# A linear-attention and squared-ReLU kernel: batch 0's attention in halves of the heads, batch 1's turns moved from TensorE to DMA, and one of batch 2's loads made to wait

## The chip, the cores and the metric

The kernel runs on one core of a Trainium2 chip. The metric is the device time of one execution in microseconds, the median of several runs. TensorE is called PE, VectorE DVE, ScalarE ACT, GpSimd POOL, and SyncE (which here only issues DMAs) SP.

## The reference

The inputs are q, k and v of 8 batches, 8 heads, 576 positions and 64 channels, and two weights, w1 (512 x 2048) and w2 (2048 x 512), all in float32. Position s has the angle pi/2 * s/576.

```python
def phi(x, c, s):                       # c, s: cosine and sine of the position
    r = np.maximum(x, 0.0)
    return np.concatenate([r * c, r * s], axis=-1)          # 128 features a head
q_p, k_p = phi(q, cos_w, sin_w), phi(k, cos_w, sin_w)
kv  = np.einsum('bhsf,bhsd->bhfd', k_p, v)
z   = np.sum(k_p, axis=2)
num = np.einsum('bhsf,bhfd->bhsd', q_p, kv)
den = np.einsum('bhsf,bhf->bhs', q_p, z)[..., None] + 1e-06
x   = (num / den)                        # heads side by side: 4608 rows of 512
h   = x @ w_in
r   = np.maximum(h, 0.0)
out = (r * r) @ w_out
```

## The kernel before

Work goes by batches. A batch has 576 positions: four tiles of 128 (j = 0 to 3) and a tail of 64 (j = J = 4). Its attention is made of these steps, each a declared operation:

- loads: `k`, `v`, `q` of the batch, 1 MB each, and their tails `kt`, `vt`, `qt`, two transfers of 64 KB each. There is one buffer for each name, so a batch's load waits until the batch before has read it.
- features: for every j the cosine half and the sine half of k and of q (`relu_scale`, L407 on DVE, L405 on ACT), and a cast of v to bfloat16 beside a column of ones (`vx`, L412).
- the product of k's features and v with its ones, `kz`, summed over j, and a copy of it, `kvz`.
- the turn of q's features, so that the feature lies on the partitions: for batches 2 to 7 by DMA transposes on SP (`declare_qT`, L567), for batch 1 and batch 0 by PE against an identity with a copy out of PSUM (`declare_qT_pe`, L580; in the prologue L1107).
- numerator and denominator in one product, `num`, and the division on DVE (`div`, L626 to L628).
- the turn of the result x to `xT`: for batches 2 to 7 by DMA transposes (`declare_xT`, L656), for batch 1 and 0 by PE (`declare_xT_pe`, L668; prologue L1135).

After it come the first product of the two-layer part, `x @ w1`, its ReLU on ACT and square on DVE, and the second product with w2. Batches 0 to 2 do the first product plainly (`declare_plain`); batch 0 does the second one by rows (`declare_rows`, 64 matmuls of 512 columns, which use w2 quarter by quarter); later ones use a scheme with seven block products in place of eight. Almost all matmuls are recorded at L429, the helper `mm`.

The order on the engines is not written by hand, except for the prologue. Every operation is declared with the engines that may do it, its duration, what it reads and writes, and for PE a place in time (`pos`). A planner then walks through time: it picks on each engine what can start first, and among equals what is due first, gives out the buffers, and so makes a fixed instruction order for each engine. `SHIFTS`, a string of "operation number : shift", moves the due times of single operations, and sometimes fixes an engine. On the chip every engine works through its list in order and waits where it must. Operations called `given` tell the planner when something that it does not place itself will be ready.

Before the planner's part stands `prologue` (L1057), written out by hand: it issues batch 0's loads (k on SP, the others on POOL's queue), the constants, the four loads of w1 (L372, `load_w1`), and does the attention of batch 0's first two tiles for all heads at once. While PE has nothing to do, it is kept busy by matmuls on zeros (L1069, L1101, L1132), whose results nobody reads. Tiles 2, 3 and the tail of batch 0 are declared for the planner. POOL's queue then loads w2 in quarters (L379) and batch 1:

```python
    declare_load(1, "q", "POOL", 17.0)
    declare_w2_load(0, 19.0, 10.0)
    declare_load(1, "k", "POOL", 20.0)
    declare_w2_load(1, 22.0, 11.0)
    declare_load(1, "v", "POOL", 23.0)
    declare_w2_load(2, 25.0, 12.0)
    declare_w2_load(3, 26.0, 13.0)
```

and after batch 1's attention, in the declared order, batch 2's q, k and v, also on POOL. w1 and w2 are converted to bfloat16 by the transfer. Batches 3 to 7 are loaded from SP.

Of the kernel before, what the change touches and what calls it, by code (L numbers as in the profile page):

```python
# [21 lines left out]
21:4.5 31:1.0 44:-3.0 53:1.5 60:1.0 74:3.0 80:2.0 93:-7.5 105:-0.5 132:-2.5 134:2.0 146:-7.0  # L22
149:-8.5 153:-6.5:ACT 178:4.0 181:-2.5 192:32.0 198:-6.0 206:3.0 215:-1.5 236:3.0 252:18.5
255:10.5 257:20.5 260:-2.5 261:18.5 263:3.0 264:-1.0 296:-16.5 300:-26.0 313:4.0 315:-1.5
335:-1.5 339:-6.0 350:-3.5 390:5.0 392:4.0 411:3.5 440:66.0 446:-7.5 467:6.5:DVE 470:13.5:DVE
486:-2.5 500:3.0 527:4.0 559:1.5 566:1.0 569:1.0 571:0.5 575:3.5 578:-2.0 581:-2.0 583:1.0
587:3.0 608:-3.5 609:1.0 619:-1.5 620:8.5 625:4.5 628:9.0 632:-49.0 644:-1.0 646:1.5:ACT 653:1.0
670:8.5 675:9.0 683:5.5 700:2.5 725:-4.0 727:-4.5 729:2.5 731:6.0 755:-4.5 759:-2.5 761:-1.5
762:-2.0 777:6.0 783:1.0 789:-1.0 799:-3.0 804:3.0 806:-5.0 807:-5.0:ACT 810:-5.5:ACT 814:33.5
818:-5.5 827:8.0 828:-29.5 833:5.5 835:-9.5 848:-7.0 854:12.5 873:0.5 913:-2.0 915:1.5 927:3.5  # L30
928:13.5 947:1.5 955:-15.0 964:-3.0 973:4.0 1003:-25.5 1005:4.0 1010:4.0 1012:4.5 1015:2.0
1036:5.0 1072:11.5 1151:7.0 1156:9.0 1169:-3.5 1218:2.5 1278:-1.5 1330:-1.0 1335:3.0
# [18 lines left out]
class Planner:  # L51
# [23 lines left out]
    def add(self, engs, fn, r=(), w=(), pos=None, lat=None, size=None, after=(), land=2.2, held=None):  # L75
# [5 lines left out]
        op.land, op.held = land, held  # L81
# [45 lines left out]
    def plan(self, t0):  # L127
# [7 lines left out]
        for o in pe:  # L135
            o.late = o.slot = t
            t += o.engs["PE"]
# [37 lines left out]
        while left:  # L175
# [32 lines left out]
            if o.size:  # L208
                pipe = max(o.end + o.land, pipe) + o.size
                o.done = pipe + self.margin  # L210
                if o.held is not None:
                    o.end = max(o.end, pipe - o.held)
# [19 lines left out]
def kernel(  # L232
# [120 lines left out]
    def load_main(src, nm, i, b, eng, parts=1):  # L353
        main = mem[nm][:, i]
        for n in range(parts):
            js = slice(n * J // parts, (n + 1) * J // parts)
            eng.dma_start(
                out=main[:, :, js, :],
                in_=src[b, :, 0:MAIN, :].rearrange("h (p j) d -> p h j d", j=J)[:, :, js, :],
            )  # L360
# [74 lines left out]
    LOAD = 3.4  # L435
# [10 lines left out]
    T1, T2, t = {}, {}, 16.8  # L446
# [11 lines left out]
    def declare_load(b, nm, eng, pos=None, after=()):  # L458
        src = {"k": k, "v": v, "q": q}[nm]
        queue = nc.sync if eng == "SP" else nc.gpsimd  # L460
        for part, fn, cost, size in ((nm, load_main, 0.7, LOAD), (nm + "t", load_tail, 1.4, 0.4)):
            buf = loaded[part, b] = plan.buf(part)

            def load(_, fn=fn, buf=buf):
                fn(src, nm, buf.i, b, queue)

            add((eng, cost), load, w=[buf], pos=pos, size=size, after=after)

    def source(nm, b, j):
        return loaded[nm if j < J else nm + "t", b]  # L470

# [27 lines left out]
    def declare_feature(nm, b, j, part, engs):  # L499
# [4 lines left out]
        cost = {"ACT": 0.63 * n, "DVE": 0.40 * n}  # L504
# [5 lines left out]
        add({e: cost[e] for e in engs}, feature, r=[source(nm, b, j)], w=[(buf, j % 2, part)])  # L510
# [11 lines left out]
    def declare_kz(b, pos, engs=("ACT",)):  # L522
        ba, bb = plan.buf("F"), plan.buf("F")
        kvz = kvzb[b] = plan.buf("kvz")
        for j in range(NS):

            def kz(_, j=j):
# [18 lines left out]
                ("PE", T_MM65 * (2 * HH)),  # L546
# [47 lines left out]
    def declare_num(b, j, pos):  # L594
# [22 lines left out]
        add(("PE", T_MM65 * 2 * HH), num, r=[qT, kvzb[b]], w=bks, pos=pos)  # L617
# [75 lines left out]

    def declare_plain(b, hb, half, pos, split=False):
# [3 lines left out]
        for c in range(2) if split else (None,):  # L698

            def plain(_, c=c):  # L700
# [13 lines left out]
                r=[(xT, i) for i in ((0, 1) if c is None else (c,))] + [("w1", hb // 4)],  # L714
# [77 lines left out]
    def declare_seven1(b, r, t):  # L792
# [12 lines left out]
        def product(name, off, acc, w, x, first, reads):  # L805
# [27 lines left out]
            ("DVE", 0.6), lambda _: add_relu(block(1, 1), halves(bank(E)), halves(at(u3))),  # L833
# [4 lines left out]
            ("DVE", 0.6), lambda _: add_relu(block(0, 1), halves(bank(E)), halves(at(u2))),  # L838
# [65 lines left out]
    def declare_pair(b, pair, t):  # L904
# [7 lines left out]
        for n, ops, op, reads in (  # L912
# [5 lines left out]
            add(("DVE", 0.6), lambda _, n=n, ops=ops, op=op: sub(at(gs[n]), *ops(), op), r=reads, w=[gs[n]])  # L918
# [92 lines left out]
    def declare_att(b, kpos, npos, cos_k="B", cos_q="D", cast="A"):  # L1011
        EN = {"B": BOTH, "A": ACT1, "D": DVE1}
        cos_k, cos_q, cast = (EN.get(x, x) for x in (cos_k, cos_q, cast))
# [5 lines left out]
        for j in range(NS):  # L1019
            declare_feature("q", b, j, "c", cos_q)  # L1020
            declare_feature("q", b, j, "s", ACT1)
            if b > 1 and (j == J or j % 2):
                declare_qT(b, j // 2)
            elif b == 1:
                declare_qT_pe(b, j, npos[j] - 3.5, DVE1)
        for j in range(NS):
            declare_num(b, j, npos[j])
            if b > 1 and (j == J or j % 2):
                declare_xT(b, j // 2)
            elif b == 1:  # L1030
                declare_xT_pe(b, j, npos[j] + 2.0, BOTH)
# [10 lines left out]
    loaded["k", 0] = bind(plan.buf("k"), 0, 9.5)  # L1042
    loaded["v", 0] = bind(plan.buf("v"), 0, 12.0)
    loaded["q", 0] = bind(plan.buf("q"), 0)
    loaded["kt", 0] = bind(plan.buf("kt"), 0, 9.5)
    loaded["vt", 0] = bind(plan.buf("vt"), 0, 12.0)
    loaded["qt", 0] = bind(plan.buf("qt"), 0)
    for j in range(NS):
        bind(kp_of(0, j), j if j < J else 0, 12.5)
        bind(cached(vxb, (0, j), "vx" if j < J else "vxt"), j if j < J else 0, 12.5)  # L1050
    kvzb[0] = bind(plan.buf("kvz"), 0)
    bind(qp_of(0, 0), 0, 13.6)
    bind(x_of(0, 0), 0, 16.8)
    bind(xT_of(0, 0), 0)
    qTp0 = [bind(plan.buf("qpTp"), j, 14.6) for j in range(2)]

    def prologue():  # L1057
        nc.vector.memset(zeros, 0.0)
        for t, n in (("vx", D), ("vxt", D)):
            m = mem[t]  # L1060
            nc.vector.memset(m[:, :, :, D:E1], 1.0)
        load_main(k, "k", 0, 0, nc.sync)
        load_tail(k, "k", 0, 0, nc.gpsimd)
        load_main(v, "v", 0, 0, nc.gpsimd)
        load_tail(v, "v", 0, 0, nc.gpsimd)
        constants()
        load_main(q, "q", 0, 0, nc.gpsimd, 2)
        for i in range(31):
            nc.tensor.matmul(out=banks[:, i % 2, :], lhsT=zeros[:, 0:P], rhs=zeros, start=True, stop=True)  # L1069
        for j in range(NS):  # L1070
            kp = at(kp_of(0, j))
            relu_scale("DVE", kp[:, :, 0:D], piece("k", 0, j), cos_col[:, j : j + 1])
            relu_scale("ACT", kp[:, :, D:F], piece("k", 0, j), sin_col[:, j : j + 1])
        for j in range(NS):
            copy("ACT" if j == 1 else "DVE", at(vxb[0, j])[:, :, 0:D], piece("v", 0, j))
        for i in range(4):
            load_w1(i, 4)
        load_tail(q, "q", 0, 0, nc.gpsimd)
        kz = banks[:, 6:8, :]
        for j in range(NS):  # L1080
            for hh in range(HH):
                for half in range(2):
                    h = half * HH + hh
                    kp, vx = at(kp_of(0, j)), at(vxb[0, j])
                    if j < J:
                        lhsT, rhs = kp[:, h, :], vx[:, h, :]
                    else:
                        p0, p1 = half * TAIL, (half + 1) * TAIL
                        lhsT, rhs = kp[p0:p1, hh, :], vx[p0:p1, hh, :]
# [163 lines left out]
```

## Time and profile before

| | us |
|---|---|
| runs | 279.13, 279.6, 278.8; median 279.13 |
| the profiled execution's own time | 278.33 |
| its span, first to last instruction | 276.6 |
| PE / DVE / ACT / POOL busy | 269.0 / 219.1 / 192.6 / 28.4 |
| granted clock of PE | 1.00 |
| first matmul with w1 starts | 18.49 |
| last matmul ends | 272.6 |

Busy times are sums of recorded instructions; matmuls overlap in the pipeline, so their spacing, as the chain of waits gives it, says more than their recorded durations of some 0.2 to 0.3 us. In the chain a matmul of 128 columns takes 0.056 us, and eight of 256 columns take 0.87 us. The DMA's "busy share" can exceed 1 in a window, since more than one packet of an engine can be under way.

In the first 18 us the engines work on batch 0's attention, and the loads landed as follows (time of issue and time to landing by the trace): k 6.25, v 9.8, q's two halves 11.46 and 12.98, the quarters of w1 at 16.1, 18.0, 20.5 and 23.1. Then on the same queue: the first w2 quarter at 26.8, batch 1's q at 29.4, its k at 32.0, the second w2 quarter at 34.4, batch 1's v at 37.6, the third and fourth w2 quarter at 40.7 and 43.3, batch 2's q, k and v at 46.2, 49.2 and 52.6.

### The profile page before, as it was taken

The numbers are of one execution on the slowest core, as the hardware profiler recorded it, in microseconds if no ns is written. First come the engines' busy times: TensorE is split into PE (matmuls) and PEld (weight loads), VectorE is DVE, ScalarE is ACT, GpSimd is POOL, SyncE is SP. The second block draws the span as 40 slices with busy tenths as digits, with TensorE's granted clock in tenths as the row PEclk, the third lists the DMA queues.
The fourth block names the chain that finished last, engine by engine and source line by source line (L and its number), as shares of the span: only waits on it lengthen the run. The fifth ranks groups of instructions, "written<-read, shape, count | busy, mean of one in ns | idle before, by whom it ended". The sixth has DMA issues, their size and how long they took to land.

```text
span 276.6 us, 7125 instructions
## 1 busy us (share of the span) xinstructions
PE 269.0 (97%) x2846; PEld 227.8 (82%) x2851; DVE 219.1 (79%) x515; ACT 192.6 (70%) x385; POOL 28.4 (10%) x46
## 2 busy tenths in 40 slices
PE   8979999999999999999999999999999999999994
PEld 3658856789888988888888888988988888888883
DVE  1849996998795896799977999799946997279741
ACT  3767862798798796499848995699738643685421
POOL 8925244100000000000000000000000000000000
PEclk9999999999999999999999999999999999999999
DMA  7999999776999999899899428997583301200024
GB/s 228 311 206 287 330 256 374 220 174 148 368 191 257 281 248 238 220 331 160 237 266 377 114 40 167 330 219 210 57 233 77 94 32 42 112 1 2 8 88 134
DMA packets 77824, 53.01 MB, mean 192 GB/s; under 512 B 52032, under 2 KB 73024, under 8 KB 77792
## 3 DMA queue, kind: packets, MB, share of 16 engines
q1 hardware_dynamic: 70368, 37.63, 54.7%
q0 software_dynamic: 7280, 14.81, 19.8%
q8 instruction: 22, 0.36, 0.5%
q10 hardware_dynamic: 144, 0.13, 0.1%
q14 instruction: 10, 0.08, 0.1%
HBM read 36.70 MB, written 9.44 MB: 167 GB/s over the span
## 4 chain that ended last, share of the span: by engine, by line
PE 81%; DVE 11%; DMA 2%; issue 2%; POOL 2%; ACT 1%; POOLq 0%; DVEq 0%
PE banks L429 78%; DVE gT L418 3%; DVE rs L421 3%; DVE gs L426 3%; DMA q<-in_q_dram 2%; PE banks L580 1%; DVE gTt L418 1%; PE banks L668 1%; PE banks L1132 1%; ACT qp L405 1%; POOL kt L365 1%; DVE x L628 1%; POOL vt L365 0%; ACT sums L412 0%; DVE kp L407 0%
## 5 line engine op out<-in xcount | busy, mean ns | idle before, releaser
L429 PEld LDWEIGHTS <-w1sb 128*128 128x128 bf16 x784 | 72.7, 98 | 8.7
L429 PE MATMUL banks<-xT,w1sb 128*128 128x256 bf16 (+1 forms) x576 | 68.3, 267 | 0.1
L429 PEld LDWEIGHTS <-gs 128*128 128x128 bf16 x512 | 49.5, 98 | 7.0 <-DVE gs L426 0.7
L429 PE MATMUL banks<-w2sb,gT 128*128 128x256 bf16 (+1 forms) x284 | 44.8, 295 | 0.2 <-issue 0.2
L429 PEld LDWEIGHTS <-gT 128*128 128x128 bf16 x400 | 37.4, 98 | 7.5
L415 ACT ACTIVATE rt<-banks 128x512 bf16<-128x512 f32 x64 | 37.2, 602 | 9.2 <-PE banks L429 4.5
L429 PEld LDWEIGHTS <-w1s 128*128 128x128 bf16 x320 | 30.6, 98 | 3.9 <-issue 0.2
L429 PE MATMUL banks<-w2sb,gs 128*128 128x256 bf16 x256 | 32.7, 273 | 0.1
L429 PE MATMUL banks<-w2s,gs 128*128 128x256 bf16 x256 | 32.1, 273 | 0.1
L421 DVE CUSTOM_DVE_ANT_0 rs<-banks,sums 128x512 bf16<-128x512 f32 x40 | 27.0, 684 | 3.8 <-ACT sums L829 3.1
L418 DVE TENSOR_TENSOR gT<-rs 128x1024 bf16<-128x1024 bf16 (+1 forms) x50 | 28.0, 580 | 1.2 <-ACT rs L415 0.6
L426 DVE TENSOR_TENSOR ysb<-banks,sums 128x256 f32<-128x256 f32 x32 | 13.5, 422 | 17.6 <-PE banks L429 9.4
L418 DVE TENSOR_TENSOR gT<-rt 128x512 bf16<-128x512 bf16 x48 | 19.4, 420 | 7.1 <-ACT rt L415 7.0
L415 ACT ACTIVATE rs<-banks 128x512 bf16<-128x512 f32 x40 | 23.5, 606 | 2.0 <-PE banks L429 1.8
L405 ACT ACTIVATE kp<-k,sin_col 128x512 bf16<-128x512 f32 x32 | 22.4, 725 | 0.5 <-DMA k<-in_k_dram 0.5
L429 PE MATMUL banks<-xT,w1s 128*128 128x256 bf16 x160 | 22.7, 273 | 0.0
L429 PE MATMUL banks<-xs,w1s 128*128 128x256 bf16 x160 | 22.7, 273 | 0.0
L405 ACT ACTIVATE qp<-q,sin_col 128x512 bf16<-128x512 f32 x32 | 22.0, 720 | 1.0 <-DMA q<-in_q_dram 1.0
L426 DVE TENSOR_TENSOR gs<-gT 128x1024 bf16<-128x1024 bf16 x28 | 19.2, 689 | 3.1 <-PE banks L429 2.7
L628 DVE TENSOR_TENSOR x<-banks,den 128x512 bf16<-128x512 f32 x30 | 20.7, 691 | 1.0
L429 PE MATMUL banks<-xTt,w1sb 128*128 128x256 bf16 x128 | 16.1, 273 | 0.0
L407 DVE TENSOR_SCALAR kp<-k,cos_col 128x512 bf16<-128x512 f32 x26 | 12.0, 501 | 5.0 <-DMA k<-in_k_dram 5.0
(105 smaller groups left out, 362.8 us busy)
## 6 DMA issues: line engine op xcount, KB each, us to landing
out_dram<-ysb SPq DMA_DIRECT2D x13, 512.0 KB, 3.6
k<-in_k_dram SPq DMA_DIRECT2D x6, 1024.0 KB, 6.4
v<-in_v_dram SPq DMA_DIRECT2D x5, 1024.0 KB, 7.5
q<-in_q_dram SPq DMA_DIRECT2D x5, 1024.0 KB, 9.3
v<-in_v_dram POOLq DMA_DIRECT2D x3, 1024.0 KB, 8.2
w1sb<-in_moe_w_in_dram POOLq DMA_DIRECT2D x4, 512.0 KB, 10.9
w2sb<-in_moe_w_out_dram POOLq DMA_DIRECT2D x4, 512.0 KB, 12.4
q<-in_q_dram POOLq DMA_DIRECT2D x2, 1024.0 KB, 9.1
```

Source lines behind the costliest of these rows:

```text
L365: eng.dma_start(out=tail[g * TAIL : (g + 1) * TAIL, :, :], in_=src[b, g * HH : (g + 1) * HH, MAIN:S, :].rearrange("h p d -> p h d"),)
L405: nc.scalar.activation(out=dst, in_=src, func=ACTF.Relu, scale=col)
L407: nc.vector.tensor_scalar(out=dst, in0=src, scalar1=0.0, scalar2=col, op0=ALU.max, op1=ALU.mult)
L415: nc.scalar.activation(out=out, in_=in_, func=ACTF.Relu)
L418: nc.vector.tensor_tensor(out=out, in0=in_, in1=in_, op=ALU.mult)
L421: nc.vector._custom_dve(TENSOR_ADD_SAT, out=out, in0=in0, in1=in1, s0=float("inf"), s1=0.0)
L426: nc.vector.tensor_tensor(out=out, in0=in0, in1=in1, op=op)
L429: nc.tensor.matmul(out=out, lhsT=lhsT, rhs=rhs, start=start, stop=stop, skip_group_check=True)
L580: nc.tensor.transpose(t[:, h, :], qp_at(b, j)[:, h, :], ident[:, :])
L628: nc.vector.tensor_tensor(out=x_at(b, j).rearrange("p (b k) (l d) -> p b k l d", b=n, l=2), in0=n4[:, :, :, 0:D].rearrange("p b (k l) d -> ...
L668: nc.tensor.transpose(t[:, kb, :], x_at(b, j)[:, kb, :], ident[:, :])
L1132: nc.tensor.matmul(out=banks[:, 6 + i % 2, :], lhsT=ident[:, :], rhs=zeros, start=True, stop=True)
```

## The change

1. *Batch 0's loads* are all issued from SP's queue in one order: k, k's tail, the first half of q (tiles 0 and 1), v's tail, v's heads 0 to 3, v's heads 4 to 7, the second half of q, q's tail. POOL makes both feature halves of k's tile 3. A one-element copy on POOL, from v's first half into w1's buffer, stands ahead of the four w1 loads, so these, and all behind them on POOL, are issued when that half of v has landed.
2. *Batch 0's first two tiles* are declared for the planner (`declare_first`) rather than written out, and in two halves g of the heads: casts of v, products `kz` (the tail first), the copy `kvz`, numerators, divisions and the turns of x are each made for heads 0 to 3 and heads 4 to 7 apart. The planner starts at 8.0 on PE in place of 16.8. Fill matmuls on zeros: 28 ahead and 7 between.
3. *Batch 1* is turned like the later batches, by DMA transposes on SP: two of q's main tiles and one of the tail, the same for x. Its 36 q transposes and 18 x transposes on PE go, with their copies.
4. *POOL's loads* are in another order: w2 quarter 0, batch 1's q, w2 quarter 1, batch 1's k and v, w2 quarters 2 and 3, then batch 2. In the instruction order as built batch 2 follows as k's tail, q, q's tail, v, v's tail, and k's main load last; ahead of that one stands a one-element copy on POOL that reads batch 1's x, tiles 2 and 3, so it is issued after batch 1's last main division.
5. Several planner durations and all of `SHIFTS` are new, so the order of later stages changes on every engine too.

```diff
 SHIFTS = """
-21:4.5 31:1.0 44:-3.0 53:1.5 60:1.0 74:3.0 80:2.0 93:-7.5 105:-0.5 132:-2.5 134:2.0 146:-7.0
...
+7:-0.5 22:3.0:ACT 31:1.5 59:5.0 65:-1.0 68:6.0 71:-3.0 80:0.5 85:-2.0 130:14.5 135:1.0 143:2.5
...
-        for part, fn, cost, size in ((nm, load_main, 0.7, LOAD), (nm + "t", load_tail, 1.4, 0.4)):
+        for part, fn, cost, size in ((nm, load_main, 0.7, size), (nm + "t", load_tail, 1.4, 0.4)):
             buf = loaded[part, b] = plan.buf(part)
 
             def load(_, fn=fn, buf=buf):
+                if gate and fn is load_main:
+                    nc.gpsimd.tensor_copy(out=at(buf)[0:1, 0, 0, 0:1], in_=x_at(*gate)[0:1, 0, 0:1])
                 fn(src, nm, buf.i, b, queue)
...
-            if b > 1 and (j == J or j % 2):
+            if j == J or j % 2:
                 declare_qT(b, j // 2)
-            elif b == 1:
-                declare_qT_pe(b, j, npos[j] - 3.5, DVE1)
         for j in range(NS):
             declare_num(b, j, npos[j])
-            if b > 1 and (j == J or j % 2):
+            if j == J or j % 2:
                 declare_xT(b, j // 2)
-            elif b == 1:
-                declare_xT_pe(b, j, npos[j] + 2.0, BOTH)
...
     def prologue():
+        for src, nm, part in (
+            (k, "k", 0), (k, "kt", 0), (q, "q", 0), (v, "vt", 0), (v, "v", 0), (v, "v", 1), (q, "q", 1), (q, "qt", 0)
+        ):
+            if nm[1:]:
+                load_tail(src, nm[0], 0, 0, nc.sync)
+            elif nm == "k":
+                load_main(src, nm, 0, 0, nc.sync)
+            elif nm == "q":
+                load_main(src, nm, 0, 0, nc.sync, [slice(part * J // 2, (part + 1) * J // 2)])
+            else:
+                h = slice(part * HH, (part + 1) * HH)
+                nc.sync.dma_start(
+                    out=mem["v"][:, 0, h],
+                    in_=v[0, h, 0:MAIN, :].rearrange("h (p j) d -> p h j d", j=J),
+                )
...
-        load_main(k, "k", 0, 0, nc.sync)
-        load_tail(k, "k", 0, 0, nc.gpsimd)
-        load_main(v, "v", 0, 0, nc.gpsimd)
-        load_tail(v, "v", 0, 0, nc.gpsimd)
         constants()
-        load_main(q, "q", 0, 0, nc.gpsimd, 2)
-        for i in range(31):
-            nc.tensor.matmul(out=banks[:, i % 2, :], lhsT=zeros[:, 0:P], rhs=zeros, start=True, stop=True)
...
+        fill(28)
+        for c, col in ((0, cos_col), (D, sin_col)):
+            nc.gpsimd.tensor_scalar(
+                out=at(kp_of(0, J - 1))[:, :, c : c + D], in0=piece("k", 0, J - 1),
+                scalar1=0.0, scalar2=col[:, J - 1 : J], op0=ALU.max, op1=ALU.mult,
+            )
+        nc.gpsimd.tensor_copy(out=w1sb[0:1, 0, 0:1], in_=mem["v"][0:1, 0, 0, 0, 0:1])
         for i in range(4):
             load_w1(i, 4)
-        load_tail(q, "q", 0, 0, nc.gpsimd)
...
+    ORDER1 = []
+    pos = 21.0
+    for nm in "0q1kv23KQV":
+        if nm != "-":
+            ORDER1.append((pos, nm))
+        pos += 1.0 if nm == "-" else 2.65 if nm in "0123" else 3.1
...
+    def declare_transfers(order):
+        for pos, nm in order:
+            if nm in "kvqKVQ":
+                b = 2 - nm.islower()
+                declare_load(b, nm.lower(), "POOL", pos, size=2.7, gate=(1, 3) if nm == "K" else None)
+            else:
+                declare_w2_load(int(nm), pos, 10.0)
...
-    t0 = {"PE": 16.8, "ACT": 17.3, "DVE": 17.1, "SP": 10.0, "POOL": 20.0, "GIVEN": 0.0}
+    t0 = {"PE": 8.0, "ACT": 6.3, "DVE": 6.3, "SP": 10.0, "POOL": 14.2, "GIVEN": 0.0}
```

The core of `declare_first`, for one half g of the heads (casts, product, copy; numerators, divisions and turns of x follow in the same manner):

```python
        for g in range(2):
            hs = slice(g * HH, (g + 1) * HH)
            for i in range(2):                      # cast(): v's heads hs, tiles 2i and 2i + 1
                add({"ACT": 0.6, "DVE": 0.55}, cast, r=[(L("v"), g)],
                    w=[(vxb[0, j], g) for j in (2 * i, 2 * i + 1)])
            for j in (J, *range(J)):                # kz(): four products, one a head
                add(("PE", T_MM65 * HH + 0.02), kz,
                    r=[(kp_of(0, j), j % 2, c) for c in "cs"] + [(vxb[0, j], g) if j < J else vxb[0, j]],
                    w=[ks[g]], pos=12.0 + g + 0.01 * ((j + 1) % NS))
            add({"ACT": 0.35, "DVE": 0.4}, kvz_copy, r=[ks[g]], w=[(kvzb[0], g)])
```

## The prediction

> **What bounds the kernel now.** I read the page's first two parts, then PE's waits and the chain, then the DMA windows, because the change moves work from PE to the DMA queues.
>
> ```profile
> PE 269.0 (97%) x2846; PEld 227.8 (82%) x2851; DVE 219.1 (79%) x515; ACT 192.6 (70%) x385; POOL 28.4 (10%) x46
> PE   8979999999999999999999999999999999999994
> DMA  7999999776999999899899428997583301200024
> ```
>
> PE is busy in every slice after the first few, and the DMA engines are full at the same time for the first 50 us. The stretch from PE's first batch product work to its last matmul:
>
> ```profile
> 18.03:272.65 254.62, 253.93 (x2728) 220.18 (x2732) 209.23 (x489) 182.72 (x368) 16.36 (x23) 1.00 0.74 189
> ```
>
> The first two numbers are the stretch and PE's busy time: 0.7 us of idleness in 254.6. So from 18.03 on only fewer PE instructions can save time; ahead of it an earlier start can. The chain there, and PE's one real wait:
>
> ```profile
> 17.25 0.73 ACT qp L405
> 17.99 0.05 issue
> 18.03 0.62 PE banks L580 x8
> 18.65 1.34 PE banks L429 x24
> 19.99 0.45 PE banks L580 x8
> ...
> PE banks L580 <- ACT qp L405: 1.3, 1, 1.3
> ```
>
> PE stands still for 1.3 us because a q transpose is queued ahead of the first w1 product and its sine half is late on ACT. Eight transposes take 0.45 us in the chain, so 0.056 us each.
>
> The DMA side, 14 to 38 us, then a single large transfer transpose alone on the ring (53.4 to 56.0) and a pair in sequence (88 to 90):
>
> ```profile
> DMA  9999999999999999999999999999999999999999
> DMA packets 4121, 6.67 MB, mean 278 GB/s; under 512 B 240, under 2 KB 3254, under 8 KB 4118
> ...
> DMA packets 2070, 0.52 MB, mean 201 GB/s; under 512 B 2070, under 2 KB 2070, under 8 KB 2070
> ...
> DMA packets 1974, 0.50 MB, mean 249 GB/s; under 512 B 1974, under 2 KB 1974, under 8 KB 1974
> ```
>
> No slice is free between 14 and 38 us. A q transpose (0.52 MB in 256 B packets) fills all engines for 2.0 (88 to 90) to 2.6 us (53.4 to 56). And the load that matters later:
>
> ```profile
> 29.65 0.76 POOL L379 DMA_DIRECT2D w2sb<-in_moe_w_out_dram  x1 [1.97 <-DMA q<-in_q_dram]
> w2sb<-in_moe_w_out_dram POOLq DMA_DIRECT2D x1, 512.0 KB, 11.0
> ...
> 44.32 1.46 PE L429 MATMUL banks<-w2sb,gT 128*128 128x512 bf16 x6
> ```
>
> The third quarter of w2 is issued at 29.65 and lands 11.0 later, at 40.7; PE first uses it in the group at 44.3. So 3.6 us of slack.
>
> **What the Trainium skill says.** "DMA: Bandwidth & Descriptors", section "Queues, rings and completion order": an engine alternates between queues packet by packet, draining a packet of several descriptors before it switches. No window of this trace has a transpose and a POOL load both backed up, so the share each gets is unknown here. Its "Rules for kernel authors" says that issuing from several engines adds no bandwidth, since all share the same 16; the full windows agree. "TensorE: Matmul & The Clock Gate", "Part 1: The HAM clock gate": PE falls to half clock after about 3.4 us of idleness; the trace shows a clock of 1.00 throughout, with no such gap to test it. "Part 4: PE-mode transpose": its output lies in PSUM and needs a copy; the trace shows them (0.69 us on DVE for eight heads).
>
> **The change part by part.**
>
> *Batch 1's transposes.* PE loses 32 + 4 q transposes and 16 + 2 x transposes: 54 x 0.056 = 3.0 us, all of it on the path (PE idles 0.7 in 254.6). Their copies go too (DVE about four of 0.69 and some of 0.41, ACT two or three of 0.58); hidden under PE, worth nothing by themselves.
>
> *Head.* Batch 0's loads all go to SP's queue, in order of need, v in two halves of heads. My chain: k lands at 6.25 as before. Half a megabyte takes 1.5 us (q's two halves landed at 11.46 and 12.98), a tail pair some 0.5. So with k's tail, half of q and v's tail ahead, the halves of v land at 6.25 + 0.5 + 1.5 + 0.5 + 1.5 = 10.3 and at 11.8 (before v landed whole at 9.8), the rest of q at 13.3, its tail at 13.8. The first half is cast by 11.1, multiplied and copied by 12.4; the second is cast by 12.9, its product done by 13.5. Then ACT's queue decides: kv copy 0.4, two q sines 1.33, x copy 0.3, tail sine 0.5, the 8-head copy 1.0, x copy 0.3 = 17.3, so the first w1 product starts at about 17.4, against 18.03 for PE's queue head before. By then PE has also done 16 transposes and 8 numerator products that before came after 18.03: 0.90 + 0.24 = 1.14. Gain 0.6 + 1.14 = 1.7. Bounds: 2.7 (if the 8-head copy's 1.0 is off the path) and 0.7 (if as much is added). The two k features on POOL (by the skill's "GPSIMD Engine Reference", section 3.1, POOL takes 1.96 times as long as DVE; with DVE's 0.57 an estimate of 1.1 us each) end by about 9, two us before use: nothing. SP issues its twelve transfers in 0.46 (main) and 0.6 to 0.7 us (tail) each, by about 8.3 and each before its turn on the engines. The fill matmuls wait for nothing and hold no one up.
>
> *Gate on w1.* POOL's tiny copy waits for v's first half, and the four w1 loads, w2 and batch 1's loads are queued behind it on POOL: issue moves from 7.96 to about 10.4. The queue is fed again about when batch 0's loads end, so what counts is the end of batch 0: the last piece of q landed at 12.98, and now the q tail is ahead of w1 too, at 13.8. All of w1, w2 and batch 1 come 0.8 later, 1.0 with some slip at the change of queue. The last w1 quarter, landed at 23.1, then comes at 24.1 where PE would want it at 17.4 + 6.2 = 23.6: 0.5 lost, but absorbed by the next wait.
>
> *Transfers for batch 1.* Added on SP: two q transposes (2.0 to 2.6 us of all engines each), a small one (0.5), and for x half of that. They start when batch 1's q (29.4 before, about 30.5 now) has its features, about 32 to 34, in the middle of the full stretch, and ahead of them POOL still has k, v and half of w2 to bring. The three q transposes cost 4.5 to 5.7 if nothing overlaps. The third w2 quarter lands at 40.7 + 1.0 + (0 to 5.7) = 41.7 to 47.4. I take 3.5 of it, 45.2: the last transpose partly falls behind that quarter, and POOL's cast loads leave a little room. PE wants that quarter earlier than before: 44.3 - 1.7 (head) - 1.34 (24 q transposes gone) + 0.48 (two numerators now ahead) = 41.8. It waits 45.2 - 41.8 = 3.4. Batch 1's v is on the same queue just ahead and gates PE's kv product likewise; its wait lies inside this one. Behind the waiting PE stand the rows, the numerators, batch 1's divisions, and its x transposes.
>
> *Hold on batch 2.* Only k's main load waits for the division; q and v are ahead of it in POOL's queue, and behind it only two stores. With the last w2 quarter at about 48, three loads at 2.6 each (the distance of such landings before: q 29.4, k 32.0), and x's transposes of about 2.2, k lands near 58; PE's first product with it was at 68.3, now 67. Nothing. ACT has a batch 2 q sine queued ahead of the last row copy, so a late q would block it: 0 to 1.6, taken as 0.
>
> *The new shifts* reorder every later stage. PE's idleness there is already tiny, so at best 0.3, at worst 1.5; taken as 0.
>
> **Sum:** -3.0 - 1.7 + 3.4 = **-1.3 us** on the profiled execution: 278.33 becomes 277.0 (span 276.6 to 275.3). The median of the runs is 279.13, 0.8 above that execution, so 277.8.
>
> **Rivals.** (1) *The transfers ride free*: loads and transposes overlap, the quarter lands at 42, and 0.3 of waiting is left. Gain 4.7 - 0.3 = 4.4, 274.7. For: the engines move 278 GB/s at full busy, and up to 400 in other windows. Against: busy is full either way. (2) *Strictly additive*: the quarter lands between 46.5 and 47.4, the wait is 4.7 to 5.6, and the gain is eaten: 0 to +0.9, 279.5. (3) *Starved transposes, slower*: if a ring with large packets keeps the engines, the w2 quarter comes early, at about 43 (wait 1.3), and q's second transpose, wanted 1.3 later, at 44.4, stays behind v, the rest of w2 and batch 2's q. It decides from a landing at about 47.8, where both waits together reach the 4.7 gained; at 50 they are 1.3 + 5.6 = 6.9, net +2.2, and half clock after such a gap some 0.8 more: +3.0, 282.1. For: queues full; q and v of batch 2 are not held. Against: many small tail loads on POOL's queue give turns to SP's. (4) *The hold does nothing*: k would have come last anyway; 0 either way, inside the above.
>
> **How the numbers follow.** Case 1 has 0.20; my case 0.33 (of it 0.05 within the bound); additive 0.12, of it 0.10 within; starved or a later stage upset 0.35. A measurement of this kernel can tell about 0.3% (0.8 us) from no change. Faster 0.20 + 0.28 = 0.48, same 0.15, slower 0.35 + 0.02 = 0.37. My case alone spans 276.3 to 278.8; the range to 274.6 and 282.0 leaves out about 0.08 below and 0.12 above.
>
> **What would show it.** Right: L580 and L668 fall by 36 and 18; the first w1 product near 17.4; PE waiting 3 to 4 us between 38 and 47, ended by v's casts and the w2 quarter landing near 45; little idleness after. Wrong: no such wait (case 1), or the wait ended by a q or x transpose and PE's clock below 1.00 afterwards (case 3), or new PE idleness after 70 us.

## The result: 6.5% slower, and the profile after

The changed kernel takes 298.52 us (median of 4 runs, 295.97 to 301.88) against 279.37 for the kernel before (4 runs, three of them in the table above): a ratio of 1.065, with an interval of 1.057 to 1.073. Its slowest run and that of e7_no_hold (310.47), each over 1.5% above the fastest of its kernel, are left out of ratios and intervals, and differences from the changed kernel are taken below from the median of its other three runs, 297.99. The profiled execution took 297.99 too, with a span of 295.9 against 276.6, so 19.3 us are to be explained.

The page of the changed kernel, its first two parts:

```profile
PE 268.0 (91%) x2788; PEld 225.4 (76%) x2793; DVE 218.5 (74%) x514; ACT 189.8 (64%) x380; POOL 28.2 (10%) x41
PE   8879980239999999999999999999999999999994
PEclk9999995557999999999999999999999999999999
DMA  7999999993999999998977894799539700110024
```

PE has lost 58 of its recorded matmuls, 54 of them the turns, and is otherwise as busy as before, except in three slices of 7.4 us each, from 44 to 66: there it is 0 to 30% busy, and its granted clock falls to half. The DMA engines are as busy there as anywhere. PE's waits name the cause:

```profile
PE banks L429 <- DMA qpT<-qp: 18.4, 2, 13.8
PE banks L429 <- DMA w1sb<-in_moe_w_in_dram: 1.7, 2, 1.3
```

Two waits, 18.4 us together, for batch 1's q transposes, the transfers that the change put in the place of PE's turns. PE's timeline (start, duration, line, tiles, in brackets the idle time before and its releaser) and SP's queue place them:

```profile
18.96 3.72 PE L429 MATMUL banks<-xT,w1sb 128*128 128x128 bf16 x48 [1.30 <-DMA w1sb<-in_moe_w_in_dram]
...
57.19 1.06 PE L429 MATMUL banks<-kvz,qpT 128*128 128x65 bf16 x16 [13.81 <-DMA qpT<-qp]
...
65.35 0.62 PE L429 MATMUL banks<-kvz,qpT 128*128 128x65 bf16 x8 [4.54 <-DMA qpT<-qp]
```

```profile
33.90 25.50 SPq L574 DMA_TRANSPOSE qpT<-qp  x2
```

SP issues the first q transpose at 33.90. It lands at 57.1, 23.2 us later. The second is issued at 42.77, since SP's queue is held by the first for 8.7 us, and lands at 65.27. In the kernel before, batch 2's first q transpose landed 4.4 us after its issue, and the slowest of all twelve 6.8. The DMA windows 34 to 38, 38 to 46, 48 to 64 and 64 to 66, in this order (queue q0 holds POOL's loads, q1 the transposes; packets, MB, share of the 16 engines):

```profile
q0 software_dynamic: 426, 1.54, 102.8%
...
q0 software_dynamic: 1041, 1.28, 90.4%
q1 hardware_dynamic: 990, 0.25, 33.9%
...
q0 software_dynamic: 698, 2.40, 62.3%
q1 hardware_dynamic: 2148, 0.54, 55.0%
...
q1 hardware_dynamic: 1991, 0.49, 118.3%
```

From 34 to 38 no packet of the transpose moves at all. From 38 to 46 both queues send about as many packets, but a packet of the transposes has 256 bytes and one of the loads 1.2 KB on average. From 48 to 64 it is another picture: three packets of the transposes to one of the loads, and both are slow, 2.94 MB in 16 us, or 184 GB/s, where the loads alone moved 385 from 34 to 38. These views do not show what holds both there. From 64, when batch 2's q and v have landed (60.8 and 64.0), the transposes get the engines for themselves and move twice as many packets in 2 us as in the 8 us from 38 to 46. PE's clock, in windows (length, PE busy, ..., the last three numbers are clock, DMA share, GB/s):

```profile
66.00:68.00 2.00, 2.00 (x6) 0.71 (x5) 1.06 (x3) 0.00 (x0) 0.00 (x0) 0.50 0.03 6
68.00:70.00 2.00, 2.00 (x14) 0.98 (x13) 0.92 (x3) 0.00 (x0) 0.00 (x0) 0.61 0.00 0
70.00:72.00 2.00, 2.00 (x17) 0.91 (x16) 1.75 (x6) 0.12 (x1) 1.47 (x2) 1.00 0.33 66
```

After the second landing PE works for 4.2 us at half clock (65.35 to about 69.6), which loses about 2.1 us. At 57 to 61 it is slow too, but waits afterwards anyway.

The stretches 43 to 82 and 110 to 270 show where PE stands still:

```profile
43.00:82.00 39.00, 20.38 (x173) 13.18 (x172) 15.41 (x40) 10.47 (x20) 7.17 (x11) 0.69 1.00 176
110.00:270.00 160.00, 159.77 (x1736) 141.96 (x1734) 134.85 (x301) 121.09 (x247) 0.00 (x0) 1.00 0.71 181
```

In the first PE is idle for 18.6 us (0.2 in the kernel before), in the second for 0.2 (0.3 before), and from 18 to 43 for 1.4 (0.2 before). The added idleness and the half clock, less the 3.0 us that the turns are estimated at, make 18.7 of the 19.3 us.

Last the head. POOL's cosine feature, its copy and its first w1 issues:

```profile
6.62 2.35 POOL L1078 TENSOR_SCALAR kp<-k,cos_col 128x512 bf16<-128x512 f32 x1 [4.75 <-DMA k<-in_k_dram]
11.34 0.18 POOL L1082 CAST w1sb<-v 1x1 bf16<-1x1 f32 x1
11.82 1.77 POOL L372 DMA_DIRECT2D w1sb<-in_moe_w_in_dram  x2 [0.31 <-POOL w1sb L1082]
```

The two features take 2.35 and 2.41 us, w1 is issued from 11.82 on, its first quarter lands at 18.83, and PE's first w1 product starts at 18.96, against 18.49 before.

### The profile page after: what moved, and what is told of

It is laid out like the page before. It is cut to its first block, busy times and chain, and to the rows that moved or that the text cites. A ratio compares the mean times of both kernels' runs of the same rounds, so it can differ in the third digit from the quotient of the medians.

```text
span 295.9 us, 7023 instructions
## 1 busy us (share of the span) xinstructions
PE 268.0 (91%) x2788; PEld 225.4 (76%) x2793; DVE 218.5 (74%) x514; ACT 189.8 (64%) x380; POOL 28.2 (10%) x41
## 4 chain that ended last, share of the span: by engine, by line
PE 71%; DMA 13%; DVE 10%; POOL 3%; issue 1%; ACT 1%; DVEq 0%; POOLq 0%
PE banks L429 71%; DMA qpT<-qp 8%; DMA w1sb<-in_moe_w_in_dram 3%; DVE gT L418 3%; DMA k<-in_k_dram 2%; DVE w1s L426 2%; POOL kp L1078 2%; DVE rs L421 1%; DVE x L635 1%; DVE kp L407 1%; POOL w1sb L372 1%; DVE qp L407 1%; POOL kt L365 0%; DVE den L634 0%; DVE w2s L426 0%
## 5 line engine op out<-in xcount | busy, mean ns | idle before, releaser
L429 PEld LDWEIGHTS <-gT 128*128 128x128 bf16 x400 | 38.6, 99 | 11.3 <-issue 2.7
L429 PE MATMUL banks<-w2sb,gT 128*128 128x256 bf16 (+1 forms) x284 | 46.5, 307 | 0.3 <-issue 0.2
L429 PE MATMUL banks<-kvz,qpT 128*128 128x65 bf16 x224 | 11.6, 201 | 18.4 <-DMA qpT<-qp 18.4
L633 DVE TENSOR_SCALAR den<-banks 128x8 f32<-128x8 f32 (+1 forms) x38 | 6.1, 160 | 29.9 <-PE banks L429 29.6
L429 PEld LDWEIGHTS <-qpT 128*128 128x128 bf16 x224 | 10.6, 102 | 20.4 <-DMA qpT<-qp 19.4
L429 PE MATMUL banks<-xs,w1s 128*128 128x256 bf16 x160 | 23.5, 273 | 0.0
L426 DVE TENSOR_TENSOR ysb<-banks,sums 128x256 f32<-128x256 f32 x32 | 13.4, 420 | 13.6 <-PE banks L429 8.9
L429 PE MATMUL banks<-xT,w1s 128*128 128x256 bf16 x160 | 22.5, 273 | 0.0
L426 DVE TENSOR_TENSOR gs<-gT 128x1024 bf16<-128x1024 bf16 x28 | 19.3, 688 | 2.0 <-PE banks L429 1.6
L405 ACT ACTIVATE qp<-q,sin_col 128x512 bf16<-128x512 f32 x30 | 20.7, 719 | 0.0
## 6 DMA issues: line engine op xcount, KB each, us to landing
k<-in_k_dram POOLq DMA_DIRECT2D x2, 1024.0 KB, 11.8
```

Of the source, the lines that this page charges most:

```text
L405: nc.scalar.activation(out=dst, in_=src, func=ACTF.Relu, scale=col)
L426: nc.vector.tensor_tensor(out=out, in0=in0, in1=in1, op=op)
L429: nc.tensor.matmul(out=out, lhsT=lhsT, rhs=rhs, start=start, stop=stop, skip_group_check=True)
L633: nc.vector.tensor_single_scalar(out=d, in_=n4[:, :, :, D], scalar=EPS, op=ALU.add)
```

## The experiments

Theory A: a transpose on SP's queue and loads on POOL's queue share the engines packet by packet, so a transpose beside backed-up loads (loads that have packets waiting all the time) gets few bytes, PE waits for it, and then runs at half clock. The rivals: the new order of batch 0 and of the later stages costs the time, or a transpose is slow under load whatever is queued.

**e1_turn_pe.** The changed kernel with batch 1 turned by PE again:

```diff
-            if j == J or j % 2:
+            if b == 1:
+                declare_qT_pe(b, j, npos[j] - 3.5, DVE1, extra=True)
...
+            elif j == J or j % 2:
                 declare_qT(b, j // 2)
...
-    declare_att(1, T2[0] + 4.5, [T2[0] + 6.5 + 1.0 * x for x in range(NS)], DVE1, DVE1, DVE1)
+    declare_att(1, T2[0] + 4.5, [T2[0] + x for x in (6.0, 9.0, 12.0, 14.0, 19.0)], DVE1, DVE1, DVE1)
```

and the same for x. The last line gives batch 1's numerators the places of the kernel before; `extra` keeps the numbers that `SHIFTS` refers to, so the shifts hold for the same operations. The planner still makes a new order of what follows.

> The changed kernel with one part undone: batch 1's q and x are turned on PE again, with the turn positions of the kernel before; the head in halves, the load order and the hold stay. Theory A (the transposes starve on SP's ring while POOL's ring is full, and PE waits for them): the 18.4 us of waiting for transposes go, and about 3 us of half clock after them; 3.0 us of PE transposes come back: 298.5 - 18.4 - 3 + 3 = about 280, between 277 and 283. Rival B (the head in halves and the new order of all stages cost the time, and the transposes only show it): stays above 290.

284.67 us (283.37 to 287.36), ratio 1.022 [1.016, 1.029]; no wait for batch 1's transposes is left and the clock is 0.999. So undoing the transfers takes back 13 of the 19 us. But it is 1.7 above the range of A: what is left of the change, which the prediction put at -1.7, costs 5.8 against the kernel before. Its waits are small and many, the first two `ACT kvz` (1.8) and `ACT rt` (1.3).

**e2_before_dma1.** The reverse, the kernel before with only batch 1 turned by transfers:

```diff
-            if b > 1 and (j == J or j % 2):
+            if j == J or j % 2:
                 declare_qT(b, j // 2)
-            elif b == 1:
-                declare_qT_pe(b, j, npos[j] - 3.5, DVE1)
...
```

and the same for x.

> The kernel before with one part of the change alone: batch 1's q and x are turned by transfers on SP; head, load order and the other stages' order as before. Theory A: POOL's queue is full until about 53 us here too, so q's transposes, issued near 35, land 15 to 20 us later in place of 5, and PE waits 8 us or more: 286 to 300. Rival B: 276 to 281, since 3.0 us of PE transposes go and nothing else changes.

302.64 us (300.57 to 303.85), ratio 1.084 [1.078, 1.089], 2.6 above the range of A, with the same wait, now of three parts:

```profile
PE banks L434 <- DMA qpT<-qp: 18.4, 3, 14.9
```

A new wait of 2.3 us for a cast of v comes with it. This one part alone makes all of the loss and more, 23.8 us; beside it the other parts of the change soften the loss, the hold among them (e7_no_hold). Undone it gave back only 13, so the parts do not simply add up.

**e3_load2_sp.** The changed kernel with batch 2's loads on SP's queue, behind batch 1's x transposes, so that POOL's queue is empty sooner:

```diff
-                declare_load(b, nm.lower(), "POOL", pos, size=2.7, gate=(1, 3) if nm == "K" else None)
+                declare_load(b, nm.lower(), "POOL" if b == 1 else "SP", pos if b == 1 else None, size=2.7, after=() if b == 1 else [turned["x", 1, 1]])
```

> The changed kernel with batch 2's q, k and v issued on SP's queue, behind batch 1's x transposes, in place of POOL's queue; no gate is needed. Theory A: POOL's ring then runs empty when the last w2 quarter lands, near 47 us, and the second q transpose lands near 51 in place of 65.3: 12 to 14 us faster than the changed kernel, 284 to 288. Rival C (a transpose next to any loads is slow for the engines' sake, whichever ring they are on): no faster than 295.

The landings were as A has them: the first q transpose at 49.5, the second at 51.3, once w2's last quarter had landed at 48.6. The total was not: 304.88 us (303.15 to 305.09), outside A's range and Rival C's side of it. The edit changed the planner's order of everything behind it; new waits, 7.1 us for a q transpose near 129 and 4.1 us for a k feature near 90, took more than was won. For the total this run is inconclusive, and the next ones keep the order.

**e4_turn_pe_no_pool.** e1_turn_pe with the two k features on DVE and ACT in place of POOL:

```diff
-        for c, col in ((0, cos_col), (D, sin_col)):
-            nc.gpsimd.tensor_scalar(
-                out=at(kp_of(0, J - 1))[:, :, c : c + D], in0=piece("k", 0, J - 1),
-                scalar1=0.0, scalar2=col[:, J - 1 : J], op0=ALU.max, op1=ALU.mult,
-            )
...
```

> As the kernel with batch 1 turned on PE, and in addition the two k features of tile 3 made by DVE and ACT in place of POOL, where they took 2.35 and 2.41 us and held the w1 loads back until 11.8. If that gate sets the head: w1 is issued at about 10.6, its first quarter lands 1.2 earlier than the 18.8 of the changed kernel, and the time falls by 0.8 to 1.3 us against the kernel with POOL's features. If the engines' share decides (batch 0's loads end at 13.8 and w1 follows): same within 0.5.

284.11 us (283.98 to 284.43), 0.6 below e1_turn_pe, which its runs cannot tell from no change. The first w1 product starts at 17.78 (18.01 there), ended by w1's landing in both. Without the features POOL's copy waits for v until 10.79, and with them it started at 10.73 in e1_turn_pe:

```profile
10.79 0.44 POOL L1090 CAST w1sb<-v 1x1 bf16<-1x1 f32 x1 [8.92 <-DMA v<-in_v_dram]
```

So here v's landing keeps w1 as long as POOL's slow features do.

**e5_hold_batch2.** The order of the changed kernel untouched; one copy on POOL makes batch 2's first load wait for batch 1's second q transpose:

```diff
+                if b == 2 and fn is load_tail and nm == "k":
+                    nc.gpsimd.tensor_copy(out=at(buf)[0:1, 0, 0:1], in_=at(qpTb[1, 1])[0:1, 0, 0:1])
                 fn(src, nm, buf.i, b, queue)
```

> The changed kernel, planned order untouched; on POOL a one-element copy ahead of batch 2's first load (k's tail) reads batch 1's second q transpose, so that q and v of batch 2 are issued only when both q transposes of batch 1 have landed. Nothing is left out. Theory A (a transpose on SP's queue gets one 256-byte packet for each larger packet of POOL's backed-up queue, so it lasts as long as POOL has loads queued): the first q transpose still runs beside w2's last two quarters and lands when they have, near 49.5, the second near 51.5, PE's wait ends near 51.5 instead of 65.3; half clock still follows. 284 to 288 us against 298.5. Rival (a transpose issued under load is slow by itself, whatever is queued on POOL): landings at 57 and 65 as before, 297 to 300.

The q transposes land at 49.1 and 50.9, and SP's queue is through with both issues at 48.8:

```profile
34.31 14.47 SPq L576 DMA_TRANSPOSE qpT<-qp  x2
```

The wait falls from 18.4 to 5.3. But the total is 293.82 us (292.14 to 296.5), 4.2 below the changed kernel and 6 above the range. PE's waits show most of the reason:

```profile
PE banks L429 <- DMA xT<-x: 5.7, 1, 5.7
PE banks L429 <- DMA qpT<-qp: 5.3, 1, 5.3
```

Batch 2's loads, now released from 51.6 on, run into batch 1's second x transpose: issued at 56.4, it lands at 73.2, 16.8 us later. So it is the loads on POOL's queue that hold a transpose up, shown twice in one run: without batch 2's loads the q transposes come 8 and 14 us earlier, and the next transpose beside these loads is slow. The rival, that a transpose under load is slow whatever is queued, is out. How the engines share their time is not shown by this run.

**e6_fill_wait.** The changed kernel with PE kept busy during the two waits:

```diff
         def num(_):
+            for _n in range({0: 62, 2: 21}.get(j, 0) if b == 1 else 0):
+                nc.tensor.matmul(out=bank(bks[0]), lhsT=ident[:, :], rhs=w1sb[:, 0, 0:FP], start=True, stop=True)
             kvz, t = at(kvzb[b]), at(qT)
```

> The changed kernel; PE is given 62 and 21 extra 512-column matmuls just ahead of batch 1's first and third numerators, into the numerators' own bank, so that it does not stand idle while it waits for the q transposes. Results unchanged. If the half clock after the gap costs about 3 us (clock 0.56 in 42.8 to 66), as the accounting says: granted clock 0.99 or more over the whole span and 294.5 to 296.5 us. If the slow stretch after the gap had another cause: no change, 298 to 299.

300.13 us (296.74 to 300.63) at a clock of 0.993: no gain. But the second transpose landed 2.5 us later here (67.74), the fills ran out 3.2 us ahead of it, and the clock fell after that gap too:

```profile
68.00:70.00 2.00, 2.00 (x16) 0.90 (x13) 1.06 (x3) 0.00 (x0) 0.00 (x0) 0.71 0.30 66
70.00:72.00 2.00, 2.00 (x14) 0.88 (x12) 1.43 (x4) 0.00 (x0) 0.30 (x1) 0.50 0.00 0
```

So the half clock was not taken away where it counts, and its price of about 2 us stays as read from the windows, not shown by a run. (One of the four runs kept a clock of 0.999 and took 296.74; the other three, at 0.989 to 0.993, took 299.99 to 300.63. When its transpose landed is not on record.) One thing it does show: from the second landing to the end of the span there are 230.8 us here, and 230.6 in the changed kernel. The landing sets the end.

**e7_no_hold.** The changed kernel without the hold on batch 2's k:

```diff
-                if gate and fn is load_main:
-                    nc.gpsimd.tensor_copy(out=at(buf)[0:1, 0, 0, 0:1], in_=x_at(*gate)[0:1, 0, 0:1])
```

> The changed kernel without the copy that holds batch 2's k load for batch 1's last division; nothing else. If the hold does something (k's load then is backed up on POOL's queue behind q and v while the second q transpose of batch 1 is still running): that transpose lands 2 to 3 us later, near 68, and the time is 300 to 302 us. If the hold does nothing, as the prediction had it: within 0.5 of the changed kernel. Below it by over 1 us would mean that the hold itself costs, by bringing batch 2's k late.

302.71 us (300.81 to 310.47), ratio 1.081 [1.076, 1.086], clear of the changed kernel's interval. k's load is now queued right behind q and v, and the second q transpose comes 3.4 us later, at 68.67, near the 68 expected:

```profile
68.71 0.62 PE L429 MATMUL banks<-kvz,qpT 128*128 128x65 bf16 x8 [8.68 <-DMA qpT<-qp]
```

From there to the end: 230.7 us. The hold is worth some 3.4 us here.

**e11_turn_pe_no_hold.** The same edit on top of e1_turn_pe.

> The changed kernel with batch 1's q and x turned by PE, as in the first run, and without the copy that holds batch 2's k load for batch 1's last division. Nothing is left out. If the hold is what costs 5 us there (k's load then runs beside batch 2's q transposes, which took 14.6 us): k lands near 54, those transposes take 5 to 9 us and the time is 280 to 282. If the new order of the later stages costs it: 284 to 285 as with the hold.

282.71 us (281.58 to 285.06), ratio 1.016 [1.012, 1.020], between the two ranges and 2 us below e1_turn_pe, but the two intervals overlap. Where PE turns batch 1, the hold brings k beside batch 2's q transposes: the first of these took 14.6 us in e1_turn_pe and 11.3 here, not the 5 to 9 expected. What is left, 3.6 us over the kernel before, lies in the new head and the order as planned here: PE idles 1.2 of the 25 us from 18 to 43 (0.2 before) and 1.3 of the 160 from 110 to 270 (0.3 before). The changed kernel itself idles only 0.2 in this last stretch, so that part belongs to the order which the planner made for this run.

**e9_transpose_alone.** The disputed cost by itself.

> A kernel with nothing of the computation left (the output is filled with zeros): six 0.52 MB transposes on SP's queue, each behind the end of the one before and of its loads: alone; beside six 1 MB weight quarters (cast on the way) on POOL's queue, two of them issued ahead of it; beside four 1 MB fp32 loads on POOL's queue; beside the same four on ACT's queue; behind two such loads on SP's own queue; alone again. Theory A (packets taken in turn, 256 bytes against the load's larger ones): alone 2 to 3 us on the engines and 4 to 5 from issue; beside the weights 20 us or more or until they are nearly done (2 KB packets, eight times the transpose's bytes); beside the fp32 loads (1 KB packets, four times its bytes) about 12 us; on ACT's queue the same as on POOL's; behind two loads on its own queue it ends 2 to 3 us after them. Rival (a transpose is slow only because POOL's queue is the one that writes descriptors in software): beside ACT's queue it takes 5 to 6 us and not 12.

In the order as built each transpose stood ahead of its own stage's loads on its queue, so the stages overlap, and single stretches are read. The DMA windows 5 to 7 (alone), 19 to 25 (beside w1 and w2 on POOL's queue), 48 to 53 (beside fp32 loads on POOL's queue) and 66 to 70 and 71 to 76 (beside fp32 loads on ACT's queue, q10), and last a second window beside the fp32 loads on POOL's queue, 37 to 47:

```profile
q1 hardware_dynamic: 1515, 0.38, 102.8%
...
q0 software_dynamic: 837, 0.83, 88.5%
q1 hardware_dynamic: 958, 0.25, 37.5%
...
q0 software_dynamic: 416, 1.61, 94.1%
q1 hardware_dynamic: 414, 0.10, 10.6%
...
q10 hardware_dynamic: 1393, 1.39, 110.2%
...
q10 hardware_dynamic: 1426, 1.44, 81.3%
q1 hardware_dynamic: 1426, 0.37, 32.1%
...
q0 software_dynamic: 309, 1.19, 82.2%
q1 hardware_dynamic: 1107, 0.28, 31.5%
```

In three of the stretches, 19 to 25, 48 to 53 and 71 to 76, the counts are nearly equal: one packet of the one, one of the other. What differs is the other packet. Weights come in packets of 1 KB as written, POOL's fp32 loads in 4 KB, ACT's in 1 KB. Six us on 16 engines over 958 transpose packets are 0.100 us a packet; 5 us over 414 are 0.193; 5 us over 1426 are 0.056. A transpose of 0.52 MB is 2048 packets, 128 an engine, so at these rates its packets would take 12.8, 24.7 and 7.2 us.

Two stretches do not fit equal turns. From 66 to 70 the transpose beside ACT's loads, issued at 65.7, has no packet under way, as in the changed kernel from 34 to 38. From 37 to 47 the transpose beside POOL's fp32 loads sends 3.6 packets for each of theirs, and both are slow (148 GB/s), as in the changed kernel from 48 to 64. Why is open.

The transposes from issue to landing: 4.3 alone; 12.1 beside the weights (expected 20 or more: I had taken 2 KB packets); 21.2 beside the fp32 loads and the last weights on POOL's queue (expected 12: I had taken 1 KB packets); 10.2 for the next, beside the rest of these loads; 11.9 beside ACT's loads (A had 12, the rival 5 to 6). The last one, behind two loads on SP's own queue, landed 1.8 us after the second of them. So the rival is wrong in its number, since ACT's loads hold a transpose up too, but POOL's fp32 loads do so for nearly twice as long. Larger packets fit this; they are not the only difference, for POOL's weights, also in 1 KB packets, cost 0.100 a packet against 0.056 beside ACT's. The kind of queue and the cast were not separated.

**e8_products_first.** A step of the kernel before that the prediction had named: PE's turn of batch 0's third q tile goes behind the first two w1 products.

```diff
-        for op in plan.plan(t0):
+        order = plan.plan(t0)
+        pe = [o for o in order if "PE" in o.engs]
+        # the turn of tile 2 goes behind the first two products, and its copy right behind it
+        turn, last = pe[0], pe[2]
...
+        order = rest[:at_] + moved + rest[at_:]
+        for op in order:
             op.fn(op.eng)
```

> The kernel before, with one step moved: PE's turn of batch 0's third q tile, and its copy, go behind the first two w1 products instead of ahead of them. Nothing is left out. The wait of 1.3 us for ACT's sine at 16.7 to 18.0 then ends where the first x copy allows, about 17.3: -0.4 to -1.0 us, or 0.1 to 0.4 per cent. Rival: the products' own inputs, the x copies on ACT behind that sine, are what is late, and nothing changes.

278.77 us (277.71 to 279.61) against 279.51, ratio 0.997 [0.995, 0.999], inside the expected range. The first product starts at 16.84, and a new wait of 1.5 appears at the turn of the q tail.

**e10_two_turns_later** and **e12_tail_turn_later** go on from there: the turn of the q tail, too, goes behind the next two products.

> The kernel before with two steps moved: PE's turn of batch 0's third q tile goes behind the first two w1 products, as in the run before, and PE's turn of the q tail behind the next two products after its old place. Nothing is left out. The wait of 1.48 us for the tail's feature at 24.1 that took the place of the first one then is covered by 1.7 us of products: 277.0 to 278.0 us, 0.4 to 0.8 per cent under the kernel before. Rival: the wait moves on to w1's last quarter or to batch 1's loads, and it stays at 278.5 to 279.

In e10 the edit took hold of the wrong turn, as the next text says; 278.66, ratio 0.999 [0.997, 1.001], and the wait is still there (1.3).

> The kernel before with two steps moved: PE's turn of batch 0's third q tile behind the first two w1 products, and PE's turn of the q tail (128x128 from qpt, four of them) behind the two products that followed it. In the run labelled e10_two_turns_later the second move took hold of the x turn of the third tile instead, so the tail's turn stayed ahead of the products and its wait of 1.29 us too. Nothing is left out. If that wait is covered now: 277.0 to 277.8 us, some 0.5 to 0.8 per cent under the kernel before. Rival: w1's last quarter, which landed at 23.5, or a later wait takes it back, and it stays at 278.5 to 279.

278.85 us (277.59 to 279.45) against 279.05, ratio 0.998 [0.996, 0.999]. The expected 277.0 to 277.8 was missed, and the rival holds. Both waits are gone from PE's list. At 25.9 PE has done 16 more of w1's matmuls than the kernel before had at 25.6, 1.4 us of lead. A new wait near 40, 0.8 us for casts of v, is where half of it goes: with the queues full until then, PE's lead turns into a wait for a load. e8 and e12 beat the kernel before by 0.2 to 0.3%, and neither is told from the other.

## Why the prediction was wrong

*What failed: the step "Transfers for batch 1".* It put the two q transposes' 2.0 to 2.6 us of all engines each on POOL's loads, as if a transpose kept its time and the loads beside it gave way, and let w2's third quarter and PE's wait for it (+3.4) carry the cost. It was the other way round. That quarter landed at 44.06, not at 45.2, and no wait for it shows. The transposes were starved: they took 23.2 and 22.5 us from issue to landing, their wait is 18.4 us, and 2.1 of half clock follow. That they starve beside the loads on POOL's queue is shown (e1_turn_pe, e2_before_dma1, e5_hold_batch2); how the engines come to share themselves out so is shown in part only (e9_transpose_alone).

*The rule was at hand.* "DMA: Bandwidth & Descriptors", section "Queues, rings and completion order", of the Trainium skill, says that an engine alternates between queues packet by packet. I cited it, and then wrote that the share was unknown. In some stretches of e9_transpose_alone the trace agrees with the page (1426 packets against 1426); in others it does not (1107 against 309), and in the changed kernel from 48 to 64 there are 2148 against 698. So equal turns would have warned of a transpose of 13 to 25 us in place of 2 to 3, but they do not account for these landings.

*Rival 3 had the mechanism, the sign and the signs to look for* (waits ended by a q transpose, clock below 1.00), but not the size. It placed the second landing at 50, from the queue of loads in front of it; it came at 65.27. Its argument against, that small tail loads give turns to SP's, does not hold: from 38 to 46 SP's queue sent about as many packets as POOL's, and it was still too little. Its 0.8 us for half clock was 2.1.

*The turns, -3.0.* The counts fell as said. No run isolates the gain, as every run that puts the turns back also gets a new order; the account by stretches above comes within 0.6 us with it.

*Head, -1.7.* The first product came at 18.96 instead of 17.4. Three terms were off: POOL's features took 2.35 and 2.41 us, not the 1.1 worked out from the skill's "GPSIMD Engine Reference", section 3.1, whose ratio of 1.96 is for another operation (here it is 4.1 times DVE's 0.57); so w1 was issued at 11.8 and not at 10.4; and I took ACT's queue for the bound, where w1 was. e4_turn_pe_no_pool shows that the first of these hardly matters. I had looked at w1's last quarter and not at its first. Landings of the kernel before were misread as well: q's second half came at 13.6 (issue 6.88 and 6.7 us to landing), not 12.98, and w1's last three quarters at 18.9, 21.4 and 24.0, not 18.0, 20.5 and 23.1.

*Hold, 0.* Wrong beside the transfers, where it is worth 3.4 us (e7_no_hold), since k's load too would then stand beside the second q transpose; it may cost 2 where PE turns batch 1 (e11_turn_pe_no_hold), which the intervals leave open.

*New shifts, 0 with a worst case of 1.5.* After 82 us this held: the changed kernel idles 0.2 us from there to 270, against 0.3 before. In e11_turn_pe_no_hold head and order together cost about 2.5 us of span, but that order is not the changed kernel's.

## What to carry to other kernels

Price a transfer that shares the engines with another queue in packets, not in bytes. A first estimate is the packets of each engine, times its own packet and the other queue's together; here it gave 12.8, 24.7 and 7.2 us where 12.1, 21.2 and 11.9 were measured, so leave room above it. A transpose of 256-byte packets that a waiting engine needs took 4.3 us alone and three to five times as long beside backed-up loads, so either hold the loads until it has landed or leave the turn on PE. And a hold only moves the collision: look for the next small-packet transfer that the released loads will meet.

## What the runs showed of the hardware that was not expected

- The same fp32 loads go in 4 KB packets from POOL's queue and in 1 KB packets from ACT's and SP's, and beside them a transpose ran at 83 packets a us in the first case (48 to 53) and at 285 in the second (71 to 76); alone it ran at 838 (5 to 6).
- A transpose issued beside backed-up loads can stand for 4 us before its first packet moves (34 to 38 in the changed kernel, 66 to 70 in e9_transpose_alone), and it held SP's queue for 8.7 us.
- In e6_fill_wait a gap of 3.2 us, by the modelled ends of matmuls, was enough for half clock; "TensorE: Matmul & The Clock Gate", "Part 1: The HAM clock gate", gives about 3.4 us. The clock fell about 1 us after work had begun again, and stayed at half until about 72. In the changed kernel it fell sooner, 2.3 us after PE's last matmul (modelled end 43.37), as the clock of the window from 45 to 46 shows: 0.84, full speed for 0.68 of it, between 1.00 and 0.50 on either side. Both times are shorter than the page's, and the measurement decides.
- POOL's feature (128x512, fp32 to bf16, one operand) took 2.4 us, about four times DVE's.
